# Query turns moved from the attention banks to the gate and value banks, and query casts dealt around the row copies, at the seam between batch 0 and batch 1

## The chip, the cores and the metric

One core of one Trainium2 chip. The metric is the device time of one execution in microseconds (us). The engines are PE (matrix products, with its weight loads shown apart as PEld), ACT, DVE and POOL (element work), and SP, which issues most DMA transfers in the order of the program. The kernel keeps matmul results in eight banks of PSUM, and writes a bank again only when an engine has copied its contents away. The clock granted to PE is given as a share of full speed. To "turn" a tile is to transpose it.

## The reference, cut to what matters

```python
kv  = einsum('bhsd,bhse->bhde', k, v)      # B=8, H=8, S=576, D=64
o   = einsum('bhsd,bhde->bhse', q, kv)
x   = o / sqrt(mean(o*o, -1) + 1e-6) * g_norm      # 4608 rows of 512
xn  = x / sqrt(mean(x*x, -1) + 1e-6) * rms_g
out = (silu(xn @ w_gate) * (xn @ w_val)) @ w_out   # d_ff = 1536
```

## The kernel before

The kernel walks through 9 blocks of 512 rows: the first 512 rows of each batch, then the tails of all eight. For each block, "up" makes 12 pairs of gate and value products (L477), silu on ACT (L482), a multiplication on DVE (L483); "down" makes the output (L519). Attention for the next block runs in between. The PSUM banks are four pools of two: gate (`g_ps`), value (`v_ps`), output (`o_ps`) and attention (`att_ps`). At the seam one gate and one value bank hold down products, and the other of each pool is free.

Batches 0 and 1 are special, since the weights are still being loaded. At the seam between them, 41 to 56 us, the down products of block 0 are cut in pieces, and batch 1's attention is put between the pieces. For that, batch 1's queries are turned by PE. Later batches' queries are turned by DMA transposes from SP (`q_rows`).

```python
class Turns:
    def q_turn(self, pair, engine):
        ps = att_pool.tile([128, NS, 2, 128], BF16, name="att_ps")
        for i in range(2):
            for j in range(NS):
                PE.matmul(ps[:, j, i, :], lhsT=bufs[self.b]["q"][...], rhs=identity,
                          is_transpose=True, ...)                     # L832
        cast(engine, self.qt[:, :, 256*pair : 256*pair+256], ps...)    # copy to SBUF
# ... the seam
att1.kv_products()                  # L286, two attention banks
for h in (0, 4):                    # casts of batch 1's queries, on ACT and DVE
    cast_heads(1, h, 2, 1, DVE); cast_heads(1, h+2, 1, 1, SC); cast_heads(1, h+3, 1, 1, DVE)
att1.kv_copy()                      # empties the two banks, ACT one, DVE one
# ... round_wo on POOL
down_part(0, 2, 4)
turns.q_turn(0, SC)
down_part(1, 2, 4)
turns.q_turn(1, DVE)
for c in range(2, 4): down_part(c, 2, 4)
# ... f_cols: state times query (L408); sums, f_o, row scales; more down_parts
down_part(0, 8, 12)
xs = [F.scale(c, F.outa[c]) for c in range(4)]
ffn.down_out(0)                     # ACT copies the output tile
alloc_q(2)
for i in range(T):                  # casts of batch 2's queries: two on ACT, two on DVE
    cast_q(2, i, SC if i < 2 else DVE)
for c in range(2): atts[2].q_rows(c)        # DMA transposes of batch 2's queries
down_part(1, 8, 12)
f_x(0, xs[0], SC); f_x(1, xs[1], SC)        # turn scaled rows (L262), copy from an attention bank
ffn.down_out(1)                     # copy, and the output DMA of row blocks 0 and 1
down_part(2, 8, 12)
f_x(2, xs[2], DVE); f_x(3, xs[3], DVE)
down_part(3, 8, 12)
for c in range(2, 4): atts[2].q_rows(c)
ffn.down_out(2); ffn.down_out(3)            # output DMA of row blocks 2 and 3
# ... block 1: up(0) ... up(4), then batch 2's state times query (L326), which needs q_rows
```

Of the kernel before, what the change touches and what calls it, by code (L numbers as in the profile page):

```python
# [11 lines left out]
BF16 = mybir.dt.bfloat16  # L12
# [8 lines left out]
def kernel(  # L21
# [20 lines left out]
    T = 4  # L42
    MAIN = 128 * T
    TAIL = S - MAIN
    NS = d_model // 128
# [5 lines left out]
    def pool(name, bufs, **kw):  # L51
        return ctx.enter_context(tc.tile_pool(name=name, bufs=bufs, **kw))
# [16 lines left out]
    gps_pool = pool("gps", 2, space=PS)  # L69
    vps_pool = pool("vps", 2, space=PS)  # L70
    ops_pool = pool("ops", 2, space=PS)
    att_pool = pool("att", 2, space=PS)
# [3 lines left out]
    PE, DVE, SC, GP = nc.tensor, nc.vector, nc.scalar, nc.gpsimd  # L76
# [25 lines left out]
    def cast(engine, dst, src):  # L102
        if engine is SC:
            engine.copy(out=dst, in_=src)  # L104
        else:
            engine.tensor_copy(out=dst, in_=src)  # L106
# [33 lines left out]
    def alloc_q(b):  # L140
        bufs[b]["q"] = qb_pool.tile([128, T, H, D], BF16, name="qb")

    def cast_heads(b, h, n, step, engine):

        src = raws[b, "q"].rearrange("p (h t d) -> p t h d", h=H, t=T)
        at = place(h)
        cast(
            engine, bufs[b]["q"][:, :, at : at + (n - 1) * step + 1 : step, :],
            src[:, :, h : h + (n - 1) * step + 1 : step, :],
        )  # L150

    def cast_q(b, i, engine):

        cast_heads(b, i, 2, 4, engine)
# [104 lines left out]
    def to_rows(x, n, c, ps, engine):  # L259

        for j in range(NS):
            PE.matmul(  # L262
                ps[:, j, :], lhsT=x[:, 2 * j : 2 * j + 2, :], rhs=identity, is_transpose=True,
                start=(j == 0), stop=(j == NS - 1),
            )
        cast(engine, xnts[n][:, :, 128 * c : 128 * c + 128], ps)
# [480 lines left out]
    xs = [A.scale(c, oA[c]) for c in range(2)]  # L747
# [9 lines left out]
    ffn = Ffn(0)  # L757
# [15 lines left out]
    xs = [Z.scale(c, oZ[c]) for c in range(2)]  # L773
# [49 lines left out]
    class Turns:  # L823
# [2 lines left out]
            self.qt = qt_pool.tile([128, NS, MAIN], BF16, name="qt")  # L826

        def q_turn(self, pair, engine):
            ps = att_pool.tile([128, NS, 2, 128], BF16, name="att_ps")
            for i in range(2):  # L830
                for j in range(NS):
                    PE.matmul(  # L832
                        ps[:, j, i, :], lhsT=bufs[self.b]["q"][:, 2 * pair + i, 2 * j : 2 * j + 2, :],
                        rhs=identity, is_transpose=True,
                        start=(i == 0 and j == 0), stop=(i == 1 and j == NS - 1),
                    )
            cast(engine, self.qt[:, :, 256 * pair : 256 * pair + 256], ps.rearrange("p j i t -> p j (i t)"))
# [46 lines left out]
    def f_x(c, x, engine):  # L884
        bank = att_pool.tile([128, NS, 128], BF16, name="att_ps")
        to_rows(x, 1, c, bank, engine)
# [3 lines left out]
    def down_part(c, lo, hi):  # L890
        ffn.down_products(c, lo, hi, pools[c])
# [38 lines left out]
    f_o(3)  # L930
    down_part(0, 8, 12)
    xs = [F.scale(c, F.outa[c]) for c in range(4)]
    ffn.down_out(0)
    alloc_q(2)
    for i in range(T):
        cast_q(2, i, SC if i < 2 else DVE)
    atts = {b: Att(b) for b in range(2, B + 1)}
    for c in range(2):
        atts[2].q_rows(c)
    down_part(1, 8, 12)  # L940
    f_x(0, xs[0], SC)
    f_x(1, xs[1], SC)
    ffn.down_out(1)
    down_part(2, 8, 12)
    f_x(2, xs[2], DVE)
    f_x(3, xs[3], DVE)
# [36 lines left out]
    for n in range(1, B + 1):  # L983
        ffn = Ffn(n)
# [82 lines left out]
```

## Time and profile before

| | before |
|---|---|
| time, first three runs | 319.34, 320.76, 320.8 us |
| span of the profiled run | 317.5 us |
| PE busy, granted clock | 97%, 1.000 |
| waits of PE for another engine after 60 us | none |

The lines that matter at the seam are shown in the prediction below. One more view of the kernel before is the DMA queue of SP from 53 us (start, length of the issue, queue, line, operation, count). The last transposes go out behind the first output, and the second output follows them.

```profile
53.91 2.60 SPq L300 DMA_TRANSPOSE qt<-qb  x2
56.62 1.26 SPq L539 DMA_DIRECT2D out_dram<-o_sb  x2
57.93 3.52 SPq L300 DMA_TRANSPOSE qt<-qb  x2
61.55 2.15 SPq L539 DMA_DIRECT2D out_dram<-o_sb  x2
```

```profile
64.91 0.40 PE L326 MATMUL o_ps<-kv_all,qt 64*128 64x64 bf16 x16
```

### The profile page before, as it was taken

To read this page: it belongs to the slowest core of one execution; us is meant where nothing else is said; L and a number is where in the kernel's file an instruction comes from. 1 tells how busy PE (TensorE), PEld (TensorE's weight loads), DVE (VectorE), ACT (ScalarE), POOL (GpSimd) and SP (SyncE) were. 2 spreads that over 40 slices of the span, in tenths; PEclk is the share of its full clock that TensorE was granted. 3 is DMA by queue.
4 is the path that set the end of the run, shared out by engine and by line. 5 is a ranking of instruction groups with operands and counts; after the bars stand their busy time and mean duration, and the time that the engine had idled before them with its cause. 6 is when DMAs were issued, how large, how long until landed. Compare 5 with 4: busy or idle time off the path is not lost.

```text
span 317.5 us, 6031 instructions
## 1 busy us (share of the span) xinstructions
PE 309.2 (97%) x2371; PEld 149.9 (47%) x2371; DVE 180.5 (57%) x378; ACT 175.7 (55%) x323; POOL 21.4 (7%) x46
## 2 busy tenths in 40 slices
PE   7899999999999999999999999999999999999995
PEld 3585455444444444444444444444444444444443
DVE  3676658579339913892289327941795079504310
ACT  3577457485667465746683768376745374233321
POOL 1274350100000000000000000000000000000000
PEclk9999999999999999999999999999999999999999
DMA  7999999695369167904790489939003610230014
GB/s 277 351 387 387 376 374 343 146 280 196 94 178 369 59 145 194 359 5 113 191 375 19 100 170 231 330 68 200 2 0 61 139 66 3 59 140 3 0 33 100
DMA packets 60712, 54.95 MB, mean 173 GB/s; under 512 B 36232, under 2 KB 45708, under 8 KB 60684
## 3 DMA queue, kind: packets, MB, share of 16 engines
q1 hardware_dynamic: 60304, 53.92, 57.2%
q10 hardware_dynamic: 380, 0.66, 0.6%
q8 instruction: 18, 0.29, 0.4%
q14 instruction: 10, 0.08, 0.1%
HBM read 37.75 MB, written 9.44 MB: 149 GB/s over the span
## 4 chain that ended last, share of the span: by engine, by line
PE 84%; DMA 10%; SPq 3%; ACT 1%; POOL 1%; issue 0%; DVE 0%
PE g_ps L477 27%; PE o_ps L519 26%; PE v_ps L477 26%; DMA st<-in_q_dram 6%; DMA st<-in_moe_w_gate_dram 3%; PE att_ps L286 1%; SPq L199 1%; PE v_ps L519 1%; DMA out_dram<-o_sb 1%; PE att_ps L326 1%; POOL wg_sb L191 1%; SPq L182 1%; SPq L119 1%; PE o_ps L326 0%; PE g_ps L519 0%
## 5 line engine op out<-in xcount | busy, mean ns | idle before, releaser
L483 DVE TENSOR_TENSOR h_sb<-silu,v_ps 128x512 bf16<-128x512 bf16 x104 | 71.1, 684 | 100.4 <-ACT silu L482 68.0
L477 PE MATMUL g_ps<-xnt,wg_sb 128*128 128x512 bf16 x416 | 106.9, 379 | 0.0
L477 PE MATMUL v_ps<-xnt,wv_sb 128*128 128x512 bf16 x416 | 106.8, 379 | 0.0
L482 ACT ACTIVATE silu<-g_ps 128x512 bf16<-128x512 f32 x104 | 62.1, 597 | 70.2 <-PE g_ps L477 58.1
L519 PE MATMUL o_ps<-wo_sb,h_sb 128*128 128x512 bf16 x396 | 87.8, 379 | 0.0
L477 PEld LDWEIGHTS <-wv_sb 128*128 128x128 bf16 x416 | 40.7, 98 | 49.1
L519 PEld LDWEIGHTS <-h_sb 128*128 128x128 bf16 x420 | 40.6, 98 | 47.7 <-issue 0.4
L477 PEld LDWEIGHTS <-wg_sb 128*128 128x128 bf16 x416 | 39.6, 98 | 46.4
L104 ACT COPY o_sb<-o_ps 128x512 f32<-128x512 f32 (+1 forms) x34 | 19.7, 581 | 40.5 <-PE o_ps L519 39.7
L373 DVE TENSOR_TENSOR xna<-outa,s1y 128x512 bf16<-128x512 bf16 x28 | 17.9, 684 | 0.0
L104 ACT CAST vb<-st 128x576 bf16<-128x576 f32 x25 | 15.7, 673 | 3.7 <-DMA st<-in_v_dram 3.7
L356 DVE TENSOR_REDUCE ssq<-sqt 128x16 f32<-128x1024 bf16 x14 | 17.1, 1220 | 0.5
L356 DVE TENSOR_REDUCE ssq<-sq 128x16 f32<-128x1024 bf16 x14 | 17.1, 1220 | 0.5
L104 ACT CAST qb<-st 128x512 bf16<-128x512 f32 (+1 forms) x30 | 16.2, 602 | 2.1 <-DMA st<-in_q_dram 2.0
L104 ACT CAST kb<-st 128x576 bf16<-128x576 f32 x20 | 12.5, 673 | 0.0
L341 ACT ACTIVATE sq<-att_ps 128x512 bf16<-128x512 f32 x14 | 7.6, 594 | 4.3 <-PE att_ps L326 3.6
L355 DVE TENSOR_TENSOR sq<-sq,gsq 128x512 bf16<-128x512 bf16 x14 | 5.9, 422 | 4.9 <-ACT sq L341 4.9
L619 PE MATMUL att_ps<-kv_all 128*128 128x512 bf16 (+1 forms) x23 | 7.5, 445 | 1.2 <-DVE sel L608 1.2
L106 DVE CAST kb<-st 128x576 bf16<-128x576 f32 x12 | 5.7, 498 | 3.8 <-DMA st<-in_k_dram 3.8
L106 POOL CAST wo_sb<-st 128x512 bf16<-128x512 f32 x12 | 7.2, 632 | 7.4 <-DMA st<-in_moe_w_out_dram 7.4
L341 ACT ACTIVATE sqt<-o_ps 128x512 bf16<-128x512 f32 x14 | 7.6, 597 | 0.0
L347 ACT CAST outa<-o_ps 128x512 bf16<-128x512 f32 x14 | 7.5, 591 | 0.0
(145 smaller groups left out, 179.6 us busy)
## 6 DMA issues: line engine op xcount, KB each, us to landing
st<-in_k_dram SPq DMA_DIRECT2D x7, 1152.0 KB, 10.2
st<-in_v_dram SPq DMA_DIRECT2D x7, 1152.0 KB, 12.3
out_dram<-o_sb SPq DMA_DIRECT2D x14, 512.0 KB, 3.1
st<-in_q_dram SPq DMA_DIRECT2D x6, 1024.0 KB, 7.8
st<-in_moe_w_out_dram SPq DMA_DIRECT2D x6, 512.0 KB, 10.4
st<-in_moe_w_gate_dram SPq DMA_DIRECT2D x4, 512.0 KB, 10.1
st<-in_moe_w_val_dram SPq DMA_DIRECT2D x4, 512.0 KB, 9.4
st<-in_k_dram SPq DMA_DIRECT2D x4, 288.0 KB, 4.1
```

Of the source, the lines that this page charges most:

```text
L104: engine.copy(out=dst, in_=src)
L106: engine.tensor_copy(out=dst, in_=src)
L341: SC.activation(out=self.in_place(self.sq[i][:, 0], g), in_=bank, func=ACT.Square)
L347: SC.copy(out=self.in_place(rows, g), in_=bank)
L355: DVE.tensor_tensor(out=sq[:, 1], in0=sq[:, 0], in1=gsq8, op=OP.mult)
L356: DVE.reduce_sum(out=self.ssq[:, c], in_=sq, axis=AX.X)
L373: DVE.tensor_tensor(out=self.xna[c], in0=self.outa[c], in1=self.alpha[:, c, :].to_broadcast([128, H, D]), op=OP.mult)
L477: PE.matmul(ps, lhsT=wt[:, s, j * 128 : (j + 1) * 128], rhs=x[:, s, :], start=(s == 0), stop=(s == NS - 1),)
L482: SC.activation(out=silu, in_=g_ps, func=ACT.Silu)
L483: DVE.tensor_tensor(out=self.h[:, j, :], in0=silu, in1=v_ps, op=OP.mult)
L519: PE.matmul(self.o_ps[c], lhsT=self.h[:, j, c * 128 : (c + 1) * 128], rhs=wo_sb[:, j, :], start=(j == 0), stop=(j == NF - 1),)
L619: PE.matmul(ps[:, 0:w], lhsT=warm_sb[:, 0:128], rhs=warm_sb[:, 0:w], start=True, stop=True, skip_group_check=True)
```

## The change

Its intent: part A turns batch 1's queries in a gate and a value bank that are free anyway, so that the first turn need not wait for the state copies. Part B moves batch 2's query casts on ACT: one into idle time ahead of the output copy, one behind the copies of the turned rows, for which PE waits. With it the output of row blocks 0 and 1 comes ahead of all four DMA transposes.

```diff
         def q_turn(self, pair, engine):
-            ps = att_pool.tile([128, NS, 2, 128], BF16, name="att_ps")
+            p, nm = ((gps_pool, "g_ps"), (vps_pool, "v_ps"))[pair]
+            ps = p.tile([128, NS, 2, 128], BF16, name=nm)
@@
+    alloc_q(2)
+    cast_q(2, 0, SC)
     ffn.down_out(0)
-    alloc_q(2)
-    for i in range(T):
-        cast_q(2, i, SC if i < 2 else DVE)
+    down_part(1, 8, 12)
+    f_x(0, xs[0], SC)
+    f_x(1, xs[1], SC)
+    for i in (1, 2, 3):
+        cast_q(2, i, SC if i == 1 else DVE)
+    ffn.down_out(1)
     atts = {b: Att(b) for b in range(2, B + 1)}
     for c in range(2):
         atts[2].q_rows(c)
-    down_part(1, 8, 12)
-    f_x(0, xs[0], SC)
-    f_x(1, xs[1], SC)
-    ffn.down_out(1)
     down_part(2, 8, 12)
```

## The prediction

> **What bounds the kernel now.** I read the page first, for the engine that fills the span.
>
> ```profile
> PE 309.2 (97%) x2371; PEld 149.9 (47%) x2371; DVE 180.5 (57%) x378; ACT 175.7 (55%) x323; POOL 21.4 (7%) x46
> PE   7899999999999999999999999999999999999995
> PEclk9999999999999999999999999999999999999999
> ```
>
> PE is busy in 97% of the span at a granted clock of 1.000 (the view of cores), and the chain that ended last is 84% PE, mostly the up and down products. So a change gains only what it takes out of PE's own gaps, and every microsecond taken out there reaches the end, because the stretch after 60 us is PE work without any wait for another engine (the list of waits, cut to PE and to after 60 us, is empty). DVE, ACT and the DMA queue matter only where PE waits for them. The change touches one stretch, batch 0's end, 41 to 56 us. There I read the timeline, one engine after the other (columns: start us, length us, engine, line, operation, count, and in brackets the idle time before it and what ended it).
>
> The first place is the turning of batch 1's queries (L832):
>
> ```profile
> 41.57 0.60 PE L519 MATMUL o_ps<-wo_sb,h_sb 128*128 128x512 bf16 x2
> 41.74 0.41 ACT L104 CAST qb<-st 128x256 bf16<-128x256 f32 x1 [1.12 <-DMA st<-in_q_dram]
> 41.75 0.63 DVE L106 CAST qb<-st 128x512 bf16<-128x512 f32 x2 [0.84 <-DMA st<-in_q_dram]
> 42.06 0.53 ACT L104 CAST kv_all<-att_ps 64x128 bf16<-64x128 f32 x2
> 42.29 0.58 DVE L106 CAST kv_all<-att_ps 64x128 bf16<-64x128 f32 x2
> 42.63 0.61 PE L832 MATMUL att_ps<-identity,qb 128*128 128x128 bf16 x8 [0.46 <-ACT kv_all L104]
> 42.64 0.43 PEld L832 LDWEIGHTS <-qb 128*128 128x128 bf16 x7 [0.74 <-DVE qb L106]
> 43.08 0.59 PE L519 MATMUL o_ps<-wo_sb,h_sb 128*128 128x512 bf16 x2
> 44.16 0.69 DVE L106 COPY qt<-att_ps 128x1024 bf16<-128x1024 bf16 x1 [1.28 <-PE att_ps L832]
> 44.91 0.41 PE L408 MATMUL att_ps<-qt,kv_all 64*64 64x512 bf16 x4
> ```
>
> The first turn needs two things: the casts of qb, which the last DMA of q releases at 41.7 and which are done at 42.38 (DVE: 41.75 + 0.63), and an attention bank, which the copy of the state by ACT frees at 42.59 (42.06 + 0.53). The bank comes last. PE stands still for 0.46 us by the brackets, 0.21 us of it after the data were there.
>
> The second place is the turning of batch 1's scaled rows (L262) ahead of the next batch's up products:
>
> ```profile
> 51.39 0.59 ACT L104 COPY o_sb<-o_ps 128x512 f32<-128x512 f32 x1 [0.28 <-PE o_ps L519]
> 51.88 1.14 ACT L104 CAST qb<-st 128x512 bf16<-128x512 f32 x2
> 52.50 1.03 PE L519 MATMUL g_ps<-wo_sb,h_sb 128*128 128x512 bf16 x4
> 52.91 1.07 ACT L104 COPY xnt<-att_ps 128x512 bf16<-128x512 bf16 x2
> 53.01 0.76 DVE L106 CAST qb<-st 128x512 bf16<-128x512 f32 x2
> 53.55 0.87 PE L262 MATMUL att_ps<-identity,xna 128*128 128x128 bf16 x8
> 53.97 0.91 DVE L106 COPY xnt<-att_ps 128x512 bf16<-128x512 bf16 x2 [0.21 <-PE att_ps L262]
> 54.26 1.03 PE L519 MATMUL v_ps<-wo_sb,h_sb 128*128 128x512 bf16 x4
> 55.12 1.03 PE L477 MATMUL g_ps<-xnt,wg_sb 128*128 128x512 bf16 x4
> ```
>
> Here lengths mislead, since matmuls overlap; starts count. Four 512-column products occupy 0.86 us from start to start (54.26 to 55.12), so after 52.50 PE is free at 53.36, but the third turn starts at 53.55, and the chain of waits has the fourth turn at 54.04 where 53.77 was possible (four transposes take 0.22, from 54.04 to 54.26). That is 0.19 + 0.27 = 0.46 us lost. Cause: the third and fourth turns need the two attention banks that ACT's two copies (52.91 to 53.98) empty, and these copies stand behind two casts of batch 2's queries, which nobody needs yet. Just before, ACT had been idle for 0.28 us.
>
> **What the Trainium skill says.** "ScalarE: Activation LUTs", section "What ACT_TABLE_LOAD costs", gives an instruction without pointer operands 186 ns + 0.833 ns per element of a row, and says that back-to-back ones overlap by about 93 ns. For 512 elements that makes 613 ns; the trace has 581 to 602 (ACT's groups of copies and casts), and the cast at 51.88 begins 0.10 us before the copy from 51.39 ends, so it agrees. "TensorE: Matmul & The Clock Gate", section "Wait — 56ns, not 53.3ns?", gives 55.6 ns for 128 columns and 215.7 for 512, start to start; the trace has 0.22 us for four and 0.86 us for four. The same page's "Architectural detail" says that PE's queue can pull a weight load ahead of matmuls in flight: one load of L832 stands at 41.80, the other seven only at 42.64.
>
> **The change part by part.** Nothing is added or removed: the order of instructions on each engine shows the same counts on PE, ACT and DVE.
>
> Part A, the turns go to the free gate and value bank. The gate bank was emptied by the last silu at 38.98, long before. What is left as a gate is qb. The heads are cast pair by pair, so the first three transposes can go by about 42.2 and the fourth waits for DVE's last cast, 42.38, plus 0.04 us for the signal: 42.42. From there five load-and-transpose pairs at 0.055 and one step to the next product: 42.42 + 6 x 0.055 = 42.75, in place of 43.08. Gain 0.33 us. Everything behind moves with it: the second turn, its DVE copy (44.16 becomes 43.83), and the L408 products (44.91 becomes about 44.58). L408 waits for that copy before and after, so its bank was never its limit. The later attention allocations keep their parity, because two of them go away.
>
> Part B, the casts are dealt around the copies. With A's shift, ACT's last row copy ends at 50.79 (50.53 + 0.59 - 0.33). One query cast now fills the idle time: 50.70 to 51.30; the output copy, ready at 51.06, runs 51.20 to 51.79; the first two turns land by 52.11 and 52.33 (52.05 + 4 x 0.055 or 8 x 0.055, the last one lasting 0.22, less 0.33); their copies run 52.15 to 52.70 and 52.62 to 53.15. PE ends the product of row block 2 at 53.36 - 0.33 = 53.03: third turn at once, fourth at 53.25, last product from 53.47, free at 54.33. All of the 0.46 us is removed. But DVE now sets the end. Its two query casts end at 53.77 - 0.33 = 53.44, its two copies last 0.91 us from about 53.46: 54.37, and with the signal the next up product starts at about 54.42 in place of 55.12. So B gives 0.46 less 0.09 = 0.37 us.
>
> Sum: 0.33 + 0.37 = 0.70 us, 0.2% of the span.
>
> **The rivals.** (1) *The later transposes take it back.* The DMA transposes of batch 2's qt now stand behind the output of blocks 0 and 1. Before, two went out at 53.91, the output at 56.62 and two more at 57.93, the last issued by 61.45. Now the output waits for ACT's second output copy, about 54.3 after one more cast, goes until 55.6, and four transposes at 1.27 to 2.2 us follow: last issue done 61.4 to 61.8. With 2.5 to 4.2 us from issue to landing (the view of tile qt) the fourth, starting about 60.4, lands at 62.9 to 64.6, and the products on it (L326) start at 64.73 - 0.70 = 64.03, its block last. The early ones had the 4 us landings, under loads of k and v that are over by then, so I expect no wait; in the worst case 0.1 to 0.5 us come back and the time is 320.2 to 320.6. (2) *Batch 2's q is not there when ACT asks 1.1 us sooner.* POOL's last wait for the output weights ended at 47.19, and q's 1 MB comes next in the queue; at 0.35 to 0.40 MB per us (the windows of 47 to 51 us) it lands near 50.0, an estimate. ACT asks at 50.7. If it landed at 51.3, the first cast would hold up the row copies and cost 0.2 us: 320.3. (3) *DVE is the limit throughout and B gives nothing*: DVE's copies were starved by PE (the bracket 0.21), and ended 0.24 us before the up product began, which speaks against it; it would leave 0.33 us, 320.4. (4) *The waits add up to more*, a second round of gaps closing between 43 and 50 us: the starts there are already one issue slot apart, so no.
>
> **Range and chances.** 320.76 - 0.70 = 320.06. The three runs before lie at 319.34 and twice at 320.8, and the profiled run took 319.51, so the spread of 1.5 us is twice the gain, and a median of three falls near one or the other end: 318.6 or 320.1. I put the value at 319.9, the range at 318.5 to 320.9. A 2% change would be 6.4 us, three quarters of all of PE's idle time (317.5 - 309.2 = 8.3 us), of which these two places hold little over one: 1% for faster, 98% for the same, 1% for slower.
>
> **What would show it.** Right: the first turn's transposes spread from about 42.0, the products after it at 42.75, no bank wait by ACT's kv_all; L408 at 44.6; ACT's qb cast before the output copy without idle time; the turns of L262 at 53.0 and 53.25 in one run of 0.61 us; the first L477 of the next batch near 54.4, released by DVE's xnt. Wrong: a new wait of L326 for DMA qt near 64 us, an ACT wait for q near 50.7, or the first L477 later than 54.8. The span of the profile should fall from 317.5 to 316.8.

## The result, and the profile after

The changed kernel took 319.5 us in the median of 6 runs (318.95 to 320.08), the kernel before 320.06 us (319.34 to 320.8) in 6. The ratio is 0.9979, with a 95% interval from 0.9958 to 1.0. A ratio here is the mean time of one kernel's fast runs over that of the other's of the same rounds, so not quite the ratio of the medians quoted. 0.9979 is 0.67 us, and the prediction had said 0.70. But the profiled run of the changed kernel was its slowest, with a span of 318.0 us where 316.8 was expected. So the agreement of two numbers is not yet an explanation.

The first place in the changed kernel, in the timeline:

```profile
41.64 0.78 PE L286 MATMUL att_ps<-vb,kb 64*64 64x64 bf16 x72
42.40 0.63 DVE L106 CAST qb<-st 128x512 bf16<-128x512 f32 x2 [0.72 <-DMA st<-in_q_dram]
42.71 0.54 ACT L104 CAST kv_all<-att_ps 64x128 bf16<-64x128 f32 x2
42.79 0.83 PE L833 MATMUL g_ps<-identity,qb 128*128 128x128 bf16 x8
44.53 0.69 DVE L106 COPY qt<-v_ps 128x1024 bf16<-128x1024 bf16 x1 [1.00 <-PE v_ps L833]
45.37 0.41 PE L408 MATMUL att_ps<-qt,kv_all 64*64 64x512 bf16 x4
```

The first turn (L833, formerly L832) starts while ACT still copies the state, 42.71 to 43.25. The wait for the bank is gone, as meant. Compared by the clock everything is later than before, because this run's start-up was slower: the last query casts begin at 42.40, where the kernel before had 41.75. Times must therefore be counted from a common event.

The second place in the changed kernel:

```profile
51.47 0.62 ACT L104 CAST qb<-st 128x512 bf16<-128x512 f32 x1
52.94 1.07 ACT L104 COPY xnt<-att_ps 128x512 bf16<-128x512 bf16 x2 [0.36 <-PE att_ps L262]
53.82 0.62 PE L262 MATMUL att_ps<-identity,xna 128*128 128x128 bf16 x8
53.90 0.63 ACT L104 CAST qb<-st 128x512 bf16<-128x512 f32 x1
54.25 0.76 DVE L106 COPY xnt<-att_ps 128x512 bf16<-128x512 bf16 x2
54.28 1.03 PE L519 MATMUL v_ps<-wo_sb,h_sb 128*128 128x512 bf16 x4
55.15 1.03 PE L477 MATMUL g_ps<-xnt,wg_sb 128*128 128x512 bf16 x3
```

The third and fourth turns (L262) are now one run of 0.62 us in place of 0.87, and ACT's row copies wait for PE (the bracket 0.36) and no longer stand behind the casts. From the last down product (54.28) to the first up product (55.15) there is 0.87 us: four products without a gap.

But the list of PE's waits has a new entry in the changed kernel, and the timeline shows it (first the list's line, then PE at the second half of the L326 products, in the kernel before sixteen in one run without a wait, at 64.91):

```profile
PE o_ps L326 <- DMA qt<-qb: 0.4, 1, 0.4
```

```profile
64.93 0.28 PE L326 MATMUL o_ps<-kv_all,qt 64*128 64x64 bf16 x8
65.58 0.29 PE L326 MATMUL o_ps<-kv_all,qt 64*128 64x64 bf16 x8 [0.37 <-DMA qt<-qb]
65.80 0.39 PE L477 MATMUL g_ps<-xnt,wg_sb 128*128 128x512 bf16 x1
```

The last eight of the 32 products stand still until the fourth transposed block of batch 2's queries has landed. The queue of SP in the changed kernel shows why that one is later:

```profile
55.04 1.26 SPq L539 DMA_DIRECT2D out_dram<-o_sb  x2
56.40 6.10 SPq L300 DMA_TRANSPOSE qt<-qb  x4
62.61 1.92 SPq L539 DMA_DIRECT2D out_dram<-o_sb  x2
```

**A common clock.** I measure from the start of the last casts of batch 1's queries on DVE, which the landing of q releases. That start varies from run to run between 41.62 and 43.27 us, whatever the kernel. From it I take three stages: to L408, to the first weight load of batch 1's up products (L477), and to the first weight load of the up products behind L326. From there to the end of the span it is 252.2 to 252.4 us in every trace but one ("54 more PE instructions" below). The span is the sum: 41.75 + 23.48 + 252.27 = 317.5 for the kernel before. All traces:

| kernel | casts start | to L408 | to first up | to up behind L326 | longest transpose packet |
|---|---|---|---|---|---|
| before | 41.75 | 3.16 | 13.16 | 23.48 | 0.45 |
| before, 2nd trace | 42.05 | 3.16 | 13.16 | 23.48 | 0.43 |
| changed | 42.40 | 2.97 | 12.53 | 23.40 | 1.70 |
| changed, 2nd trace | 41.92 | 2.97 | 12.53 | 23.19 | 1.49 |
| changed, 3rd trace | 41.66 | 2.97 | 12.53 | 22.86 | 1.17 |
| A alone | 41.62 | 2.97 | 12.97 | 23.29 | 0.42 |
| B alone | 42.59 | 3.16 | 12.72 | 23.49 | 1.61 |
| changed, transposes first | 42.54 | 2.97 | 12.53 | 22.86 | 0.19 |
| the same, 2nd trace | 42.57 | 2.97 | 12.53 | 22.86 | 0.19 |
| changed, second output held back | 43.27 | 2.97 | 12.53 | 23.17 | 1.47 |
| changed, 54 more PE instructions | 41.73 | 2.97 | 12.53 | 22.86 | 0.69 |
| transposes first, first cast back | 42.67 | 2.97 | 12.53 | 22.86 | 0.18 |
| transposes first, second cast back | 41.88 | 2.96 | 12.59 | 22.91 | 0.37 |
| transposes first, products ahead of the turns | 41.67 | 2.74 | 12.34 | 22.82 | 0.81 |

The last column is the longest time that one 256-byte packet took in this stretch, from the packet records of the trace. The four transposes consist of 2048 such packets, and the usual one takes 0.018 us.

### The profile page after: what moved, and what is told of

Read it like the earlier page. It is cut to its first block, busy times and chain, and to the rows that moved or that the text cites. A ratio compares the mean times of both kernels' runs of the same rounds, so it can differ in the third digit from the quotient of the medians.

```text
span 318.0 us, 5995 instructions
## 1 busy us (share of the span) xinstructions
PE 308.1 (97%) x2334; PEld 150.3 (47%) x2371; DVE 180.4 (57%) x378; ACT 175.7 (55%) x323; POOL 21.4 (7%) x46
## 4 chain that ended last, share of the span: by engine, by line
PE 90%; DMA 5%; SPq 1%; issue 1%; another core or an unknown queue 1%; POOL 1%; ACT 0%; DVE 0%
PE v_ps L477 28%; PE g_ps L477 28%; PE o_ps L519 26%; DMA st<-in_moe_w_val_dram 3%; DMA st<-in_q_dram 2%; PE att_ps L286 2%; PE v_ps L519 1%; PE g_ps L519 1%; PE v_ps L494 1%; DMA out_dram<-o_sb 1%; PE att_ps L326 1%; POOL wv_sb L191 1%; PE o_ps L494 1%; PE att_ps L262 0%
## 5 line engine op out<-in xcount | busy, mean ns | idle before, releaser
L477 PE MATMUL v_ps<-xnt,wv_sb 128*128 128x512 bf16 x409 | 106.2, 379 | 0.7
L477 PE MATMUL g_ps<-xnt,wg_sb 128*128 128x512 bf16 x398 | 104.6, 379 | 0.7
L519 PE MATMUL o_ps<-wo_sb,h_sb 128*128 128x512 bf16 x386 | 86.8, 379 | 0.4
L477 PEld LDWEIGHTS <-wv_sb 128*128 128x128 bf16 x416 | 40.7, 98 | 49.1
L477 PEld LDWEIGHTS <-wg_sb 128*128 128x128 bf16 x416 | 39.6, 98 | 46.4
L347 ACT CAST outa<-att_ps 128x512 bf16<-128x512 f32 x14 | 7.5, 594 | 0.0
```

The source lines that it names most:

```text
L347: SC.copy(out=self.in_place(rows, g), in_=bank)
L477: PE.matmul(ps, lhsT=wt[:, s, j * 128 : (j + 1) * 128], rhs=x[:, s, :], start=(s == 0), stop=(s == NS - 1),)
L519: PE.matmul(self.o_ps[c], lhsT=self.h[:, j, c * 128 : (c + 1) * 128], rhs=wo_sb[:, j, :], start=(j == 0), stop=(j == NF - 1),)
```

## The experiments

My theory after the first trace: A and B each take out their gap, and B's new order on the DMA queue makes the L326 wait, which gives part of it back. The rival: the wait is chance, or comes from PE being early, whatever the order. All kernels gave correct results. Those run for one look have one time only, of unknown state, since there is no second run to show whether they were slow; all runs in rounds are recorded as fast.

**A alone.** The kernel before with the three lines of `q_turn` from the change.

```diff
-            ps = att_pool.tile([128, NS, 2, 128], BF16, name="att_ps")
+            p, nm = ((gps_pool, "g_ps"), (vps_pool, "v_ps"))[pair]
+            ps = p.tile([128, NS, 2, 128], BF16, name=nm)
```

> Part A alone (the turns in the gate and value banks; the casts and the DMA order as before). Times are counted in the trace from the start of the state products of batch 1 (L286), because the start-up before it differs by up to 0.8 us from run to run. Before: the L408 products start at 4.05, the first up product of batch 1 at 14.26, the up product behind the state-times-query products (L326) at 24.38. My theory: 3.72, 13.93 and 24.05, no wait of L326 for a transpose, since the transposes go out ahead of the first output as before. Rival (the bank was only the last of several gates, and the weight loads wait for the casts anyway): 3.9 to 4.05 and 14.1 to 14.26. Time: about 0.3 us under before, not to be told from 0 by 3 rounds.

Measured from L286: L408 at 3.76, up behind L326 at 24.08, no wait of L326 for a transpose. Ratio 0.9986 (0.996 to 1.0011); 319.51 us median of 4 runs. From L286 that is 0.29 to 0.30 us, near the 0.33 expected. But L286 is the wrong zero point: q landed 0.89 us behind it before and 0.79 us here, by luck of the start-up. Counted from the casts, A is worth 3.16 - 2.97 = 0.19 us, and the same 0.19 at the next two stages (13.16 - 12.97, 23.48 - 23.29). (Most expectations below still count from L286, which lies 0.71 to 1.16 us ahead of the casts, and so name larger figures than the measured ones.)

**B alone.** The changed kernel with the old `q_turn`.

```diff
-            p, nm = ((gps_pool, "g_ps"), (vps_pool, "v_ps"))[pair]
-            ps = p.tile([128, NS, 2, 128], BF16, name=nm)
+            ps = att_pool.tile([128, NS, 2, 128], BF16, name="att_ps")
```

> Part B alone (casts dealt around the copies, transposes behind the first output; the turns in attention banks). From the start of L286: L408 at 4.05 as before, first up product of batch 1 at 13.82 (0.44 less), and then a wait of L326 for the last transposed query block of about 0.4 us, so that the up product behind it is at 24.3 to 24.4, as before: B alone gives its whole gain back. Rival (the wait seen in the changed kernel's profile came from A's shift alone, or by chance): no wait of L326, and 23.94.

Measured: to the first up product 12.72, so B takes out 13.16 - 12.72 = 0.44 us. To the up product behind L326 it is 23.49 in place of 23.48: all of it was given back at L326 in this trace, with A not in the kernel. So the wait does not need A's shift. Ratio 0.9979 (0.9949 to 1.001), 319.24 us median of 4: the times alone can't show this.

**Transposes first.** The changed kernel, with all four transposes ahead of the first output.

```diff
-    ffn.down_out(1)
     atts = {b: Att(b) for b in range(2, B + 1)}
-    for c in range(2):
+    for c in range(4):
         atts[2].q_rows(c)
+    ffn.down_out(1)
@@
-    for c in range(2, 4):
-        atts[2].q_rows(c)
```

> The changed kernel, but with all four transposes of batch 2's queries issued ahead of the first output. My theory (the order on the DMA queue made the L326 wait): first up product of batch 1 at 13.5 from the start of L286 as in the changed kernel, the last transpose lands 2 us or more before it is needed, no wait of L326, and the up product behind it at 23.65, 0.7 us under before and 0.45 under the changed kernel's profiled run. Rival (the wait comes from PE being early against the loads of batch 2, whatever the order): a wait of 0.3 us or more stays, 24.0 or later.

The queue of SP in this kernel:

```profile
54.70 5.23 SPq L300 DMA_TRANSPOSE qt<-qb  x4
60.03 3.08 SPq L539 DMA_DIRECT2D out_dram<-o_sb  x4
```

All four issues take 1.25 to 1.30 us, the two whose landing the trace has land within 2.5 us, and L326 does not wait. To the up product behind it: 22.86, which is 0.62 us less than before, and exactly A's 0.19 plus B's 0.44 (rounded). Ratio 0.9975 (0.9951 to 0.9999), 319.22 us median of 4. My theory of the order held; the rival predicted a wait here.

**Second output held back.** The question was why the last transpose took 4.3 us from issue to landing, and others 2.5. The second output and batch 3's loads wait here on a one-column copy that ACT makes behind the L326 products.

```diff
-            cast(engine or SC, self.o_sb[:, c % 2, :], self.o_ps[c])
+            if late:
+                SC.copy(out=self.o_sb[:, 1, 0:1], in_=self.o_sb[:, 1, 0:1])
+            else:
+                cast(engine or SC, self.o_sb[:, c % 2, :], self.o_ps[c])
@@
+            elif c % 2 == 1 and n == 0 and c == 3 and not late:
+                pass
@@
-        if n + 2 < B:
+        if n > 1 and n + 2 < B:
@@
+            if n == 1:
+                steps[4] += [lambda f=ffn0: f.down_out(3, late=True), lambda n=n: load_batch(n + 2)]
```

> The changed kernel, but the second output (row blocks 2 and 3) and the loads of batch 3 are held back on the DMA queue until after the L326 products, by a one-column copy of the output tile in place on ACT. In both profiled kernels the last transpose took 4.2 to 4.3 us to land and others 2.5. If the output issued behind it slows it, it lands in 2.5 us here, there is no wait of L326, and the up product behind it is at 23.7. If it is slow by what was issued ahead of it, it still takes 4 us, L326 waits 0.3 to 0.5 us, and the product is at 24.1. The whole time may be longer for the late loads of batch 3; it is not what is asked.

The output went out at 67.19 us, and still the last transpose took 4.1 us and L326 waited: 23.17 in place of 22.86. So the output behind it is not the cause. The kernel took 320.61 us in the median of 4 runs, ratio 1.0021 (0.9984 to 1.0057). I had expected that something ahead of it in the queue would be, and looked at the packet records of the trace for it. They showed something else. Here are the long packets near the last transpose in this kernel (start in us, queue, size, time in ns; not a view of the profile but its raw records):

```
63.23 q8 16384B took 1433
63.98 q1 256B took 1471
63.99 q1 256B took 1474
64.01 q1 256B took 1446
64.08 q1 4B took 1378
```

A single packet of 16 KB on queue 8 comes while the last transpose is under way, and five 256-byte packets and nine 4-byte packets take 1.2 to 1.5 us in place of 0.02. Their ends tie them to the 16 KB packet. In each of the five traces with a 256-byte packet over 1.1 us, 14 such packets (256 and 4 bytes) start over up to 0.3 us but end within 0.03 us of each other, 0.79 to 0.81 us behind the end of the 16 KB packet, whether that one took 0.93 or 1.45 us. Some other delays exist: without a 16 KB packet near, the longest 256-byte packet took 0.45 us, and 0.81 us in the kernel of the last row; I did not look for their cause. The page names queue 8; this is its line for the kernel before, and it is the same in the changed one:

```profile
q8 instruction: 18, 0.29, 0.4%
```

So these are 18 packets of the instruction stream. The Trainium skill ("Runtime: NRT & Kernel Launch", section "Instruction fetch mechanics") says that each engine's instructions come in 16 KiB blocks of 256 instructions over a DMA queue of its own. The trace agrees in the mean: in the kernel before the 18 packets lie on average 249 PE instructions apart (155 to 346 singly), and this one starts behind 1224 PE instructions before and behind 1226 in the second trace of the changed kernel. PE is the only engine with nearly that many instructions, so I take it for PE's own program. The same section calls the cost of crossing a block "mostly hidden". That speaks of the crossing itself; here the cost falls on another transfer, and the table shows the size. In four traces, of three kernels, the packet hit the transpose hard enough to make L326 wait. Take the wait as the third stage less 22.86 (for B alone less 22.86 + 0.19):

| trace | longest transpose packet | wait | difference |
|---|---|---|---|
| changed | 1.70 | 0.54 | 1.16 |
| changed, 2nd trace | 1.49 | 0.33 | 1.16 |
| second output held back | 1.47 | 0.31 | 1.16 |
| B alone | 1.61 | 0.44 | 1.17 |
| changed, 3rd trace | 1.17 | 0 | |

The wait is the stall less 1.16 us, in every one. So 1.16 us is the slack that the changed order leaves for such a stall, and the collision decides by how much it is overrun.

**The changed kernel again, one look, and then in five rounds.** No edit.

> The changed kernel itself once more, one look. So far its one trace shows L326 waiting 0.37 us for the last transpose (the next up product starts 0.49 us after the second half of L326 would have ended), with a 16 KB packet of the instruction queue among that transpose's packets. If the wait belongs to the kernel: 0.3 to 0.5 us again, and 24.1 to 24.2 from the start of the state products (L286) to the up product behind L326. If it was chance of that run: no wait and 23.6 to 23.7.

The second trace has the wait again, 0.33 us, and 319.38 us.

> The changed kernel once more, timed in five rounds. From the last query casts to the next batch's first up product 12.53 us as twice before (before: 13.16), to the up product behind L326 23.2 to 23.4 with a wait of 0.3 to 0.5 us (before: 23.48), so that the change by itself is worth 0.1 to 0.3 us; ratio 0.999, between 0.9975 and 1.0005. Rival (the 0.67 us of the first timing are the kernel's): 0.998 again.

The third trace of the same program has no wait and 22.86; my expectation of 23.2 to 23.4 was wrong. Ratio 0.9986 (0.9971 to 1.0001), which is 0.45 us; 319.08 us median of 5, before 319.82. So neither "it belongs to the kernel" nor "it was chance" is the whole: the exposure belongs to the kernel, the size to the run. In this trace PE works through L326 without a bracket:

```profile
64.19 0.40 PE L326 MATMUL o_ps<-kv_all,qt 64*128 64x64 bf16 x16
64.52 1.04 PE L477 MATMUL g_ps<-xnt,wg_sb 128*128 128x512 bf16 x4
```

**54 more PE instructions.** The changed kernel with its first warming products (matmuls at the start whose results nobody uses) cut smaller, to move the instruction packet.

```diff
-    warm(warm_ps, 9)
+    warm(warm_ps, 36, 128)
```

> The changed kernel, with its first nine 512-column warming products as 36 of 128 columns: 54 more PE instructions at the start, nothing else, the same order on the DMA queue. Theory: the 16 KB packets on the instruction queue are PE's own instruction stream (they come at the same count of PE instructions in every run), and the one near 63 us holds up the last transpose's packets for 1.5 us. With 54 more instructions ahead it comes about 2 us sooner, before the last transpose's packets; then that lands by 64.6 or so (about 3 us from its issue, not 4.1 to 4.3), L326 does not wait, and the up product behind it stands 22.9 us behind the start of the last query casts (changed kernel: 23.40 and 23.19; all four transposes first: 22.86). Rival (the order on the DMA queue alone makes the last one late): 4 us again and 23.2 to 23.4.

The packet came at 61.30, which is 19.57 us behind the casts, in place of 20.68, 19.97 and 20.09 in the three traces of the changed kernel. It moved by 0.4 to 1.1 us and not by 2. Counted in PE instructions it came behind 1276, in place of 1224 to 1228: with 54 more ahead of it, at nearly the same place in the program. So the edit did not move it as expected, and what sets its place is open. The longest transpose packet took 0.69 us and ended, like those above, 0.81 us behind the end of the 16 KB packet; the last transpose landed 3.3 us after its issue began, L326 did not wait, and the stage is 22.86. That there was no wait does not decide the theory, since one of three unedited traces had none either. The rest of this kernel took 253.1 us, not 252.2: PE ends on time, but a 19th packet comes at 311.6 us, beside the last products, and the last outputs end 0.9 us later. I did not test whether it is their cause. Time 319.7 us, one run.

**Which of the two casts matters.** Both kernels are the one with transposes first; each puts one cast back.

```diff
-    cast_q(2, 0, SC)
     ffn.down_out(0)
+    cast_q(2, 0, SC)
```

> As the kernel with all four transposes first, but the first query cast back behind the output copy; only the second cast stands behind the row copies. My theory (it is enough that one of the two casts leaves its place; ACT had 0.36 us to spare before its row copies in the changed kernel): first load of the next up products at 13.24 to 13.35 from L286, as with both moved. Rival (each cast is worth half): 13.5.

Measured 12.53 to the first up product, the same as with both moved (from L286 13.30). Time 319.82 us.

```diff
     ffn.down_out(0)
+    cast_q(2, 1, SC)
     down_part(1, 8, 12)
@@
-    for i in (1, 2, 3):
-        cast_q(2, i, SC if i == 1 else DVE)
+    for i in (2, 3):
+        cast_q(2, i, DVE)
```

> As the kernel with all four transposes first, but the second query cast ahead of the row copies, behind the output copy; only the first cast is moved, into the idle time ahead of the output copy. My theory: ACT's row copies start 0.05 to 0.1 us later than PE could feed them, the first load of the next up products at 13.3 to 13.4 from L286. Rival (each cast is worth half): 13.5.

Measured 12.59 (from L286 13.35). Time 319.17 us. Moving either cast yields nearly all of B's 0.44 us: 0.44 for the second cast alone, 0.38 for the first alone. The two halves of B are not two gains: once ACT is ahead of PE, PE's own pace is the limit.

**Products ahead of the turns.** What is left of the first gap is PE waiting for the query casts. The kernel with transposes first gives it two more products there.

```diff
     down_part(0, 2, 4)
-    turns.q_turn(0, SC)
     down_part(1, 2, 4)
+    turns.q_turn(0, SC)
     turns.q_turn(1, DVE)
```

> As the kernel with all four transposes first, and the two down products of row block 1 ahead of the first turn, so that PE has work while the last query casts run, and the turns back to back. What is left of the gap there is 0.35 to 0.4 us. My theory: L408 at 3.4 from L286 in place of 3.68, and everything behind it 0.25 to 0.3 us sooner, the up product behind L326 at 23.3; best of all kernels, about 1.1 us under before at an equal start-up. Rival (L408 then waits for ACT's and DVE's copies of the turned queries, with only two pairs of products between): L408 at 3.65 or later, nothing gained.

L408 came 2.74 us behind the casts in place of 2.97, as expected, but at the third stage only 22.86 - 22.82 = 0.04 us was left of these 0.23. The timeline of this kernel shows who took most of it (PE and DVE ahead of the next block):

```profile
53.36 1.03 PE L519 MATMUL v_ps<-wo_sb,h_sb 128*128 128x512 bf16 x4
54.35 1.02 PE L477 MATMUL g_ps<-xnt,wg_sb 128*128 128x512 bf16 x4
```

```profile
52.88 0.76 DVE L106 CAST qb<-st 128x512 bf16<-128x512 f32 x2
53.55 0.75 DVE L106 COPY xnt<-att_ps 128x512 bf16<-128x512 bf16 x2
```

From 53.36 to 54.35 is 0.99 us, so PE waits 0.13 us for DVE, whose last copy ends at 54.30. And ACT's first cast of batch 2's queries, asked for at 50.6, had to wait for the load:

```profile
ACT qb L104 <- DMA st<-in_q_dram: 0.2, 1, 0.2
```

This kernel has the lowest median of all, 318.76 us of 4 runs, ratio 0.9975 (0.9958 to 0.9992), 0.80 us under before. By the stages 0.66 us of that are its own.

**Transposes first again, in five rounds,** beside the changed kernel.

> All four transposes first, timed in five rounds beside the changed kernel. By the stages in the traces 0.62 us under before (23.48 less 22.86) and 0.3 to 0.5 under the changed kernel: ratio 0.998 to before, between 0.9965 and 0.9995, no wait of L326.

All stages repeat to 0.01 us, no wait of L326. But the ratio is 0.9992 (0.9976 to 1.0009), 319.47 us median of 6 runs, and so not below the changed kernel's 319.08 of the same rounds. The start-up varies by 1.6 us among the traces and hides 0.3 us in five rounds. That this order is better in the mean rests on the stages alone: 22.86 in both traces, where the three of the changed kernel have 23.40, 23.19 and 22.86.

**The kernel before again.** No edit.

> The kernel before once more, one look, to see whether the stage times of its one trace repeat. From the start of the last query casts of batch 1: L408 at 3.16, the first load of batch 1's up products at 13.16, the up product behind L326 at 23.48, each within 0.03 us, while the start of those casts itself may lie anywhere from 41.6 to 43.3 us. If the start-up's luck also changes the stages, these numbers move by more than 0.05.

3.16, 13.16 and 23.48, to the hundredth, with the casts 0.30 us later. Time 319.83 us. The stages belong to the kernel.

## Why the prediction was right or wrong

The time was right: 319.5 us measured, 319.9 said, range 318.5 to 320.9, "the same" within 2%. The sum at the first up product was nearly right too: 0.19 + 0.44 = 0.63 us measured, 0.70 said. Point by point:

- **PE bounds the kernel, and a gap closed at the seam reaches the end.** Right. The rest of the span was 252.2 to 252.4 us in thirteen traces of fourteen.
- **Part A, 0.33 us.** The mechanism was right, the size was not: 0.19. I had the products behind the first turn at 0.33 earlier; counted from the casts their weight load came at 1.00 (43.40 - 42.40) in place of 1.27 (43.02 - 41.75), so 0.27 to 0.28, because the fourth transpose started 0.78 us behind the start of the casts and not 0.73. Another 0.09 went at L408. Before, it started 0.06 us behind the end of DVE's copy, and in all kernels with A 0.15 us behind it. With A its weight load has two engines to wait for, DVE and ACT, and before DVE alone: the traces with A show a semaphore instruction of 0.05 us there (at 45.26 in the changed kernel) and the load 0.03 us behind it, the kernel before none. That this is the reason was not tested.
- **Part B, 0.37 us.** It was 0.44, because the term that I took off did not exist. I let DVE's two copies last 0.91 us and set the end. But these 0.91 us contained DVE's wait for the fourth turn, the very wait that the change removes. With both turns ready they lasted 0.76 us. (A slip beside it: ACT's row copies were given 0.55 and 0.53 us, and the 0.59 of the trace would end them at 52.74 and 53.21; the fourth turn at 53.25 stands.) The DVE limit appeared only in the kernel with products ahead of the turns, where PE lost 0.13 us to it.
- **Rival 1, the later transposes.** I wrote "I expect no wait", at worst 0.1 to 0.5 us. The waits were 0.54, 0.33 and 0 us in three traces. The step that failed is the one that put the 4 us landings on the early transposes, under loads of k and v. In the kernel before it was the other way round: the second landed in 2.5 us (the trace has no landing for the first), the last two in 4.0 and 4.2. I had read the minimum, median and maximum and guessed which was which. L326, which I expected to find its data there, then waited for the last transpose, which took 4.1 to 4.3 us in the two traces with a wait. The cause of the long last landing in the changed kernel, a packet of instructions (PE's own, by the counts), was not in my list at all. What lies between the end of the last transpose's data packets in the kernel before (62.36 us, just as that packet starts) and its landing at 64.4 stays open. In the second trace of that kernel the packet came at 63.15, behind the transpose's last data at 62.54, and this transpose landed in 2.54 us: the 4.2 us were not the kernel's own, and here too the packet is the suspect.
- **Rival 2, the load of batch 2's queries.** It did not hit the changed kernel, but my estimate of the landing, "near 50.0", was early: in the kernel with products ahead of the turns ACT waited for it until 50.80, with casts that start 0.08 us sooner than in the trace I estimated from. The changed kernel asked 9.07 us behind the casts, that kernel got it at 9.13. There was no margin to speak of.
- **What the change is worth.** By the stages 0.63 us less the wait: 0.08, 0.29 and 0.62 us in three traces. The timings say 0.67 and 0.45 us, with intervals that hold all of this. That the time landed on the predicted gain is therefore partly luck: the 0.67 us of the first timing are not shown to be all the change's. The kernel before also moved: its median was 320.76 us in the three runs that the sum started from, and 320.06 in the six of the result.

## What to carry to other kernels

Where a start-up varies by more than the gain, count from an event inside the trace that all later work hangs on, and compare stages: here they repeat to 0.01 us wherever PE did not wait for a transfer, while five rounds of timing could not tell 0.3 us. Before you take a duration from a row as the cost of an engine, ask whether the row contains the wait that you are about to remove. And when a change moves a transfer later, compute its slack with its own landing time, over more than one trace, not with the median's; if it is little, put the transfer that someone needs ahead of the one that nobody waits for.

## What the Trainium skill lacked or had wrong

- "Runtime: NRT & Kernel Launch", section "Instruction fetch mechanics", calls the cost of crossing a 16 KiB boundary "mostly hidden". It gives no size for what such a block can cost other transfers: here one packet of 16 KB took 0.93 to 1.45 us, 256-byte packets of a DMA transpose beside it took up to 1.70 us in place of 0.018 and ended 0.79 to 0.81 us behind it, and PE lost up to 0.54 us at the far end.
- No page that I read says that a DMA transpose issued just behind an ordinary output takes longer to issue: 2.13 to 2.23 us in place of 1.25 to 1.30 for the first one behind it (nine traces; in the five with no output ahead all four took 1.25 to 1.30). One other issue was as long, 2.11 us for the fourth transpose in the kernel with 54 more PE instructions.
